# A gated linear recurrence followed by a token and channel mixer: the order of all engines written by a list scheduler inside the kernel

## The chip, the core and the metric

The kernel runs on one core of a Trainium2 chip. Five engines work from queues of their own, each in the order in which the instructions stand in its queue: TensorE (PE) multiplies matrices, VectorE (DVE) and ScalarE (ACT) compute element by element and empty the matmul banks (PSUM), GpSimd (POOL) does slower elementwise work on SBUF and starts the weight transfers, SyncE (SP) starts the other transfers. The metric is the device time of one execution, in microseconds (us). The kernel before takes 209.94 us, the median of 3 runs (209.85 to 210.44).

## The reference

Two stages. First, for each of 4 batches and 8 heads, a recurrence over 768 tokens with a 48 x 48 state; then a mixer over tokens and over the 384 = 8 x 48 channels, with a residual around each half.

```python
for t in range(S):
    state = alpha[:, :, t, :, None] * state + np.einsum('bhd,bhe->bhde', k[:, :, t], v[:, :, t])
    y[:, :, t] = np.einsum('bhd,bhde->bhe', q[:, :, t], state)
...
xt = x.transpose(0, 2, 1)
h = np.maximum(xt @ w_tok1, 0.0) @ w_tok2
u = x + h.transpose(0, 2, 1)
h2 = np.maximum(u @ w_ch1, 0.0) @ w_ch2
return (u + h2).astype(np.float32)
```

The inputs q, k, v and alpha are float32 of 4 x 8 x 768 x 48 each (4.72 MB); the weights are 768 x 256, 256 x 768, 384 x 1536 and 1536 x 384, in float32, turned into bf16 by the transfer.

## The kernel before, in words

The recurrence is computed in chunks of 128 tokens, so that a batch is 6 chunks and the whole is 24 chunks, numbered n. A chunk loads four tiles of 128 x 384 float32 (alpha, k, q, v; `load`, L118 to L127), 196,608 bytes each, in pieces of 48 numbers per token and head, through SP's queue. Its steps are:

- `s_ln` (L129): ACT takes the logarithm of alpha.
- `s_cum` (L134): PE forms the running sums over the chunk with a triangular matrix (one wide matmul L138, four narrow ones L141). ACT forms exp of the sum and of its negative (L144, L146). POOL multiplies k by the latter (L149, tile pkk) and copies v to bf16 (L154, tile vb) and prepares the decay of the chunk for the state (L157, acqm). The product with q (L151, tile pkq) is made by DVE in the first batch and by POOL later.
- `s_tr` (L164): PE transposes pkk and pkq in eight pieces; DVE copies the result to tp in the first batch, ACT later (L171).
- `s_gt` (L174): eight matmuls give each head's 128 x 128 matrix of products; DVE applies the triangular mask (L183, gtm).
- `s_y` (L186): PE updates the state (L193, L196) in the bank pair that L180 uses too, DVE scales it to bf16 (L201), PE forms the output from the masked matrix and from the state of the chunk before (L207, L211), and ACT copies it to x (L215).

When a batch has its six x tiles, its mixer (L222) follows: `tok1` (12 matmuls, L229), `tok2` (12, L238; DVE adds x and gives u, L241), `utp` (18 transposes of u, one group for each block of 128 channels, L247 and L249), `ch1` (72 matmuls, L259, for each of 12 blocks of hidden channels the two halves of the tokens one after the other; ACT empties the first half and DVE the second, L262 and L264) and `ch2` (72 matmuls, L269, then the addition of u on DVE, L272, and the store on SP, L273). All the mixer's matmul groups rotate through three banks; the transposes of u use the bank of the chunk transposes.

The order is written by a loop over the chunks (L309 to L333). It emits the sums of chunk n+1 before the transposes of chunk n, and between the steps of a chunk it takes pieces of the mixer of an earlier batch from a queue, by a count of units. Three `ch2` groups of each batch are held back and put between the steps of the next mixer. The tile framework then orders the instructions further by its own priorities, and inserts the waits.

The transfers have an order of their own. Eight tiles of each input may be in SBUF (NIN = 8). The first chunk of the second batch has its alpha load wait for the copy vb of chunk 5 (L125 and L126). The two token weights are started by POOL after the vb of chunk 4, the two channel weights after that of chunk 5 (L313 to L318); POOL's queue is all that holds them.

## Time and profile before

| what | before |
|---|---|
| median of 3 runs | 209.94 us |
| the profiled execution's own time | 210.22 us |
| its span, first to last instruction | 208.4 us |
| PE busy, share of the span | 174.2 us, 84% |
| DVE busy | 105.0 us, 50% |
| ACT busy | 85.8 us, 41% |
| POOL busy | 62.9 us, 30% |
| HBM read and written | 25.17 MB and 4.72 MB |
| packets under 512 bytes | 100,288 of 106,322 |

The profile shows one execution. Its time is measured from outside, and is 1.8 us longer than the span from the first to the last instruction. The page cuts the span into 40 slices and gives the busy share of each engine in tenths; other views give groups of like instructions with their busy time and their waits, the waits of one engine, the instructions in order of time, and the chain of work that ended last. A line number names the line of the kernel that issued the instruction. Busy times of matmuls overlap, so the time from one start to the next says more of their cost than their own length.

### The profile page before, as it was taken

What the parts mean: (1) busy time and instruction counts of PE and PEld (TensorE: products, weight loads), DVE (VectorE), ACT (ScalarE), POOL (GpSimd) and SP (SyncE); (2) the same over time, 40 slices, a digit from 0 to 9 for tenths busy, and PEclk for the clock granted to TensorE, in tenths of its full rate; (3) what the DMA queues carried; (4) which work ended last, traced back from release to release, by engine and by line L of the source; (5) the groups of instructions that cost most, each with busy time, mean ns of one, the idle gap of its engine ahead of it and who ended that gap; (6) DMA issues with size and microseconds to landing.
All of it is one profiled execution on the core that took longest, in us unless ns stands there. A gap on an engine that the chain in (4) does not pass through costs nothing.

```text
span 208.4 us, 4139 instructions
## 1 busy us (share of the span) xinstructions
PE 174.2 (84%) x1616; PEld 111.5 (53%) x1616; DVE 105.0 (50%) x179; ACT 85.8 (41%) x171; POOL 62.9 (30%) x104
## 2 busy tenths in 40 slices
PE   1276669232799999989999999999999999999993
PEld 0154445111475566646666666667656665656661
DVE  1277554103357455438765664378656446555321
ACT  3442221040526773685167744642667310054000
POOL 2543166004450441583245234551444000000000
PEclk9999999958559999999999999999999999999999
DMA  7999939999999998999989802111100021110132
GB/s 142 220 220 212 182 40 175 208 182 198 191 222 218 188 223 167 226 237 212 235 198 220 165 1 78 39 38 42 38 5 0 35 82 38 40 39 0 38 113 75
DMA packets 106322, 26.99 MB, mean 129 GB/s; under 512 B 100288, under 2 KB 105920, under 8 KB 106304
## 3 DMA queue, kind: packets, MB, share of 16 engines
q1 hardware_dynamic: 103296, 23.60, 53.7%
q0 software_dynamic: 3008, 3.15, 9.2%
q8 instruction: 12, 0.20, 0.4%
q14 instruction: 6, 0.05, 0.1%
HBM read 25.17 MB, written 4.72 MB: 143 GB/s over the span
## 4 chain that ended last, share of the span: by engine, by line
PE 59%; issue 12%; DMA 10%; ACT 8%; POOL 6%; SPq 2%; DVE 1%; POOLq 0%; ACTq 0%
PE ps_mm L269 20%; PE ps_mm L259 19%; DMA at<-in_alpha_dram 10%; ACT tp L171 4%; PE ps_tp L169 4%; PE ps_mm L238 4%; PE gt_ps L180 3%; PE ps_tp L247 2%; PE ps_mm L229 2%; SPq L124 2%; PE ps_y L207 1%; ACT a_sb L144 1%; PE ps_cum L138 1%; PE gt_ps L196 1%; POOL vb L154 1%
## 5 line engine op out<-in xcount | busy, mean ns | idle before, releaser
L259 PE MATMUL ps_mm<-ut,wc_152 128*128 128x384 bf16 x288 | 53.4, 330 | 1.2 <-DVE rt L264 0.5
L269 PE MATMUL ps_mm<-wc_153,rt 128*128 128x384 bf16 x288 | 50.9, 326 | 0.0
L264 DVE TENSOR_SCALAR rt<-ps_mm 128x384 bf16<-128x384 f32 x48 | 26.5, 555 | 22.9 <-PE ps_mm L259 22.6
L183 DVE TENSOR_TENSOR gtm<-gt_ps,u_107 128x1024 bf16<-128x1024 f32 x24 | 29.3, 1220 | 15.7 <-PE gt_ps L180 15.7
L269 PEld LDWEIGHTS <-rt 128*128 128x128 bf16 x288 | 27.1, 98 | 16.9
L259 PEld LDWEIGHTS <-wc_152 128*128 128x128 bf16 x288 | 26.8, 99 | 17.4 <-issue 1.5
L262 ACT ACTIVATE rt<-ps_mm 128x384 bf16<-128x384 f32 x48 | 23.1, 497 | 23.8 <-PE ps_mm L259 23.8
L215 ACT ACTIVATE x_sb<-ps_y 128x384 bf16<-128x384 f32 x24 | 11.8, 492 | 39.3 <-PE ps_y L211 35.2
L272 DVE TENSOR_TENSOR o_sb<-ps_mm,u_sb 128x384 f32<-128x384 f32 x24 | 13.3, 556 | 28.7 <-PE ps_mm L269 28.7
L154 POOL CAST vb<-vt 128x384 bf16<-128x384 f32 x24 | 12.8, 532 | 35.4 <-issue 23.6
L171 ACT COPY tp<-ps_tp 128x1024 bf16<-128x1024 bf16 x18 | 18.3, 1017 | 7.0 <-PE ps_tp L169 6.7
L144 ACT ACTIVATE a_sb<-ps_cum 128x388 f32<-128x388 f32 x24 | 11.9, 495 | 18.6 <-PE ps_cum L141 13.0
L241 DVE TENSOR_TENSOR u_sb<-ps_mm,x_sb 128x384 bf16<-128x384 f32 x24 | 12.0, 550 | 14.2 <-PE ps_mm L238 14.0
L180 PE MATMUL gt_ps<-tp 48*128 48x128 bf16 x192 | 11.9, 241 | 4.6 <-DVE tp L171 2.4
L180 PEld LDWEIGHTS <-tp 48*128 48x128 bf16 x192 | 6.4, 102 | 13.6 <-ACT tp L171 5.9
L146 ACT ACTIVATE ia_sb<-ps_cum 128x384 f32<-128x384 f32 x24 | 11.7, 487 | 0.0
L149 POOL TENSOR_TENSOR pkk_128<-kt,ia_sb 128x384 bf16<-128x384 f32 x8 | 7.9, 993 | 11.7 <-ACT ia_sb L146 11.7
L238 PE MATMUL ps_mm<-ht,wt_151 128*128 128x384 bf16 x48 | 11.4, 374 | 0.0
L229 PE MATMUL ps_mm<-x_sb,wt_150 128*128 128x384 bf16 x48 | 10.1, 342 | 0.6 <-ACT x_sb L215 0.6
L207 PE MATMUL ps_y<-vb,gtm 128*128 128x48 bf16 x192 | 9.6, 192 | 0.9 <-DVE gtm L183 0.9
L151 POOL TENSOR_TENSOR pkq_125<-qt,a_sb 128x384 bf16<-128x384 f32 x6 | 6.0, 996 | 14.3 <-ACT a_sb L144 14.3
L157 POOL TENSOR_TENSOR acqm<-a_sb,bm 128x8 f32<-128x8 f32 x24 | 5.5, 230 | 14.9 <-ACT a_sb L144 13.8
(91 smaller groups left out, 204.3 us busy)
## 6 DMA issues: line engine op xcount, KB each, us to landing
at<-in_alpha_dram SPq DMA_DIRECT2D x24, 192.0 KB, 3.7
kt<-in_k_dram SPq DMA_DIRECT2D x24, 192.0 KB, 3.8
qt<-in_q_dram SPq DMA_DIRECT2D x24, 192.0 KB, 3.8
vt<-in_v_dram SPq DMA_DIRECT2D x24, 192.0 KB, 3.8
out_dram<-o_sb SPq DMA_DIRECT2D x24, 192.0 KB, 1.9
wc_152<-in_moe_w_ch_dram POOLq DMA_DIRECT2D x1, 1152.0 KB, 10.1
wc_153<-in_moe_w_ch_dram POOLq DMA_DIRECT2D x1, 1152.0 KB, 17.2
wt_150<-in_moe_w_tok_dram POOLq DMA_DIRECT2D x1, 384.0 KB, 5.3
```

The source lines that it names most:

```text
L144: act.activation(a_sb, ps_cum[:, 0 : HD + 4], AF.Exp)
L154: gates[n] = gps.tensor_copy(vb, c["vt"])
L171: (act.copy if n >= NCH else dve.tensor_copy)(tp, ps_tp)
L180: pe.matmul(gt_ps[:, 4 * (h % 2) + j, :], lhsT=tp[base : base + D, 4 + j, :], rhs=tp[base : base + D, j, :], start=True, stop=True)
L183: dve.tensor_tensor(gtm, gt_ps, mask_b, ALU.mult)
L229: pe.matmul(ps, lhsT=wt1[:, kc, m * 128 : (m + 1) * 128], rhs=x[kc], start=(kc == 0), stop=(kc == NS - 1))
L238: pe.matmul(ps, lhsT=wt2[:, kc, i * 128 : (i + 1) * 128], rhs=ht[kc], start=(kc == 0), stop=(kc == NDT - 1))
L259: pe.matmul(ps, lhsT=wc1[:, kc, mc * 128 : (mc + 1) * 128], rhs=ut[kc][:, cs], start=(kc == 0), stop=(kc == NM - 1))
L262: act.activation(t[:, cs], ps, AF.Relu)
L264: dve.tensor_scalar_max(t[:, cs], ps, 0.0)
L269: pe.matmul(ps, lhsT=rt[mc][:, i * 128 : (i + 1) * 128], rhs=wc2[:, mc, :], start=(mc == 0), stop=(mc == NDC - 1))
L272: dve.tensor_tensor(t, ps, u[i], ALU.add)
```

## The change

The loop over the chunks, the queue of mixer pieces and the framework's own ordering are taken out. In their place a class `Plan` collects every piece of work as an operation with the engines that may do it and an estimated time on each, the operations that it needs, a priority, and the buffers that it takes and frees. `issue` then walks through a model of the engines: of the operations that can start, it takes the engine whose next start is earliest and on it the one with the best priority, and emits it. The emitted order is final on every engine (`tc.manual_schedule()`); the framework still inserts the waits. In its model PE runs at half speed for the first 36 us, work of other engines counts as ready for PE 0.6 us after its end from then on, and transfers share one wire in order of issue.

With it other things change:

- Alpha and k of chunk n+1 are loaded before q and v of chunk n in the first batch. NIN is 6.
- The first token weight is started after acqm of chunk 4; the second token weight and the first channel weight after vb of chunk 5; the second channel weight after vb of chunk 6.
- A one-column copy on POOL (`hold_back`) from the second token weight into the alpha tile of chunk 6 makes that tile's load, and what follows it on SP, wait until that weight has landed.
- State updates take one of the mixer's three banks, not the bank pair of the masked matrices.
- u is transposed for two token blocks at a time into a mixer bank; the u copies go to DVE or ACT as planned, and so do tp, and the emptying of the banks after `tok1` and `ch1`.
- `ch1` runs over all 12 blocks for the first half of the tokens and then for the second; `tok1` is planned matmul by matmul, `ch2` in parts of four.
- `ch2` groups are no longer held back by hand; priorities place them.

Some of the rings of buffers are a little longer or shorter. The computation of each piece is as before.

```diff
+class Plan:
...
+    LAG = {"PE": 220, "ACT": 180, "DVE": 150, "POOL": 110}
+    def __init__(self, rings, cold, window, slack):
+        self.rings = rings
+        self.cold = cold
+        self.window = window
+        self.slack = slack
+        self.ops = []
+        self.taken = {r: [] for r in rings}
+        self.asked = {r: [] for r in rings}
+        self.mixed = ("pmix", "ptp", "pcum")
+    def op(self, engines, emit, deps=(), prio=0, takes=None, frees=(), lands=0.0):
+        o = {"eng": engines, "emit": emit, "deps": [d for d in deps if d is not None],
+             "prio": (prio, len(self.ops)), "takes": [takes] if isinstance(takes, str) else list(takes or ()), "lands": lands, "users": [],
+             "end": None}
+        for t in frees:
+            t, only = t if isinstance(t, tuple) else (t, None)
+            t["users"].append((o, only))
+        for ring in o["takes"]:
+            self.asked[ring].append(o)
+        self.ops.append(o)
+        return o
+    def issue(self):
+        free = {}
+        wire = 0.0
+        todo = list(self.ops)
+        while todo:
+            ready = []
+            for o in todo:
+                if any(d["end"] is None for d in o["deps"]):
+                    continue
+                at = max((d["end"] for d in o["deps"]), default=0.0)
+                if "PE" in o["eng"] and at > self.cold:
+                    at = max(d["end"] + (0.0 if "PE" in d["eng"] else self.slack)
+                             for d in o["deps"])
+                for ring in o["takes"]:
+                    held = self.taken[ring]
+                    if ring not in self.mixed and o is not next(
+                            p for p in self.asked[ring] if p["end"] is None):
+                        at = 1e12
+                    if len(held) >= self.rings[ring]:
+                        at = max([at] + [u["end"] or 1e12 for u, only in
+                                         held[-self.rings[ring]]["users"] if only in (None, ring)])
+                if at >= 1e12:
+                    continue
+                ways = []
+                for e, ns in o["eng"].items():
+                    start = max(at, free.get(e, 0.0))
+                    slow = 2.0 if e == "PE" and start < self.cold else 1.0
+                    ways.append((start + ns * slow, start, e))
+                done, start, eng = min(ways)
+                ready.append((start, o["prio"], eng, done, o))
+            assert ready, "a ring is too small"
+            eng = min(ready, key=lambda r: r[:2])[2]
+            mine = [r for r in ready if r[2] == eng]
+            limit = min(r[0] for r in mine) + self.window.get(eng, 0.0)
+            start, _, _, done, o = min((r for r in mine if r[0] <= limit), key=lambda r: (r[1], r[0]))
+            todo.remove(o)
+            free[eng], o["start"] = done, start
+            if o["lands"]:
+                wire = max(wire, start + 1650.0) + o["lands"]
+                o["end"] = wire + 900.0
+            else:
+                o["end"] = done + self.LAG.get(eng, 0)
+            for ring in o["takes"]:
+                self.taken[ring].append(o)
+            o["emit"](eng)
...
+    plan = Plan({"loads": NT * 4, "at": NIN, "kt": NIN, "qt": NIN, "vt": NIN, "la": NLA, "a": NAUX,
+                 "ia": NAUX, "pkq": NPK, "pkk": NPK, "vb": NAUX, "acqm": NAUX, "tp": NGT,
+                 "gtm": NGT, "ss": NSS, "x": 18, "ht": 4, "u": 12, "ut": 2, "rt": NRT,
+                 "o": 6, "pcum": 1, "ptp": 1, "pgt": 1, "py": 1, "pmix": NMIX}, 36000.0, {"PE": 0.0}, 600.0)
...
-    def after(ins, gate, cls=mybir.DependencyClass.Sync):
-        tc.add_manual_dep(ins.ins, gate.ins.name,
-                          mybir.DependencyInfo(cls, mybir.DependencyReason.DATA),
-                          reason="transfer order")
-        return ins
-
-    def load_weight(dst, src, gate):
-        after(gps.dma_start(dst, src.rearrange("(c p) m -> p c m", p=128)), gate,
-              mybir.DependencyClass.NoSync)
...
+    def weight(name, dst, src, after):
+        def emit(e):
+            gps.dma_start(dst, src.rearrange("(c p) m -> p c m", p=128))
+        wload[name] = plan.op({"POOL": 1000}, emit, [after], prio=-1,
+                              lands=dst.shape[1] * dst.shape[2] * 512 / 350.0)
...
+        loads[n][name] = plan.op({"SP": 550}, emit, [after], takes=[name, "loads"], lands=196608 / RATE)
...
+    def hold_back(landed, issued):
+        def emit(e):
+            c = tiles[NCH]
+            c["at"] = inp.tile([128, H, D], F32, name="at")
+            gps.tensor_copy(c["at"][:, 0, 0:1], wt2[:, 0, 0:1])
+        return plan.op({"POOL": 70}, emit, [landed, issued], -1)
...
+        def e_tp(e):
+            c["tp"] = gtp.tile([128, 8, 128], BF16, name="tp")
+            (dve.tensor_copy if e == "DVE" else act.copy)(c["tp"], c["ptp"])
+        tp = plan.op({"DVE": 600, "ACT": 905}, e_tp, [trk, trq], P, takes="tp", frees=[trk])
...
+            def e_su(e):
+                ps = c["s"] = ps_mix_p.tile([128, HD], F32, name="ps_mm")
+                if ci > 0:
+                    pe.matmul(ps[:, 0:HD], lhsT=idd2, rhs=s_prev, start=True, stop=False,
+                              skip_group_check=True)
+                for j in range(4):
+                    pe.matmul(ps[:, 96 * j : 96 * j + 96],
+                              lhsT=pkk_t[n % NPK][:, 2 * j : 2 * j + 2, :],
+                              rhs=c["vb"][:, 2 * j : 2 * j + 2, :],
+                              start=(ci == 0 and j == 0), stop=(j == 3), skip_group_check=True)
+            su = plan.op({"PE": 330 if ci else 170}, e_su, [pkk, vb, s_dep], P, takes="pmix",
+                         frees=[pkk, vb] + ([s_dep] if ci else []))
...
+            def e_utp(e, g=g, hold=hold):
+                hold["ps"] = ps_mix_p.tile([128, 6, 128], BF16, name="ps_mm")
+                for j in range(NM):
+                    for i in range(2):
+                        pe.transpose(hold["ps"][:, 2 * j + i, :],
+                                     u[2 * g + i][:, j * 128 : (j + 1) * 128], id128)
+            tj = plan.op({"PE": 330}, e_utp, us[2 * g : 2 * g + 2], TOK,
+                         takes="pmix" if g else ["pmix", "ut"])
+
+            def e_ut(e, g=g, hold=hold):
+                if g == 0:
+                    ut_t[0] = utpool.tile([128, NM, S], BF16, name="ut")
+                (dve.tensor_copy if e == "DVE" else act.copy)(
+                    ut_t[0][:, :, g * 256 : g * 256 + 256],
+                    hold["ps"].rearrange("p (j i) t -> p j (i t)", i=2))
+            uts.append(plan.op({"DVE": 470, "ACT": 700}, e_ut, [tj], TOK,
+                               frees=[(tj, "pmix")]))
+            if g == 0:
+                ut_op = tj
...
+        rts, heads = [], []
+        for half in range(2):
+            cs = slice(half * 384, half * 384 + 384)
...
+                c1 = plan.op({"PE": 3 * MM}, e_ch1,
+                             (uts if half else uts[0:2]) + [wload["wc1"]] + heads[-1:],
+                             CH1, takes=["pmix"] if half else ["pmix", "rt"],
+                             frees=[(ut_op, "ut")])
+
+                def e_rt(e, mc=mc, cs=cs, hold=hold):
+                    evac(e, rt[mc][:, cs], hold["ps"])
+                rts.append(plan.op(EV, e_rt, [c1], CH1, frees=[(c1, "pmix")]))
+                heads.append(c1)
...
+            first = prev = None
+            for part in range(3):
+                prev = plan.op({"PE": 4 * MM}, lambda e, part=part, f=e_ch2: f(e, part),
+                               rts + [wload["wc2"], prev], CH2 - (0.05 if part else 0),
+                               takes=None if part else "pmix",
+                               frees=[(h, "rt") for h in heads[:NDC]])
+                first = first or prev
...
-        for n in range(NT):
-            b, ci = divmod(n, NCH)
-            if n + 1 < NT:
-                s_cum(n + 1)
-            if n + 1 == NCH - 2:
-                load_weight(wt1, moe_w_tok1, gates[n + 1])
-                load_weight(wt2, moe_w_tok2, gates[n + 1])
-            if n + 1 == NCH - 1:
-                load_weight(wc1, moe_w_ch1, gates[n + 1])
-                load_weight(wc2, moe_w_ch2, gates[n + 1])
-            while n + 1 >= NCH - 1 and loaded < min(NT, n + 1 + AHEAD):
-                load(loaded)
-                loaded += 1
-            if n + 2 < NT:
-                s_ln(n + 2)
-            s_tr(n)
-            over = fill(10 + over)
-            s_gt(n)
-            over = fill(10 + over)
-            s_y(n)
-            over = fill(9 + over)
-            if ci == NCH - 1:
-                fill(1000)
-                add_mixer(b)
-                over = 0
...
+    load_ak(0)
+    for n in range(NT):
+        if n + 1 < NCH:
+            load_ak(n + 1)
+        if n < NCH:
+            load_qv(n)
+        pkk, vb, acqm = chunk(n)
+        if n == NCH - 2:
+            weight("wt1", wt1, moe_w_tok1, acqm)
+        if n == NCH - 1:
+            weight("wt2", wt2, moe_w_tok2, vb)
+            weight("wc1", wc1, moe_w_ch1, vb)
+        if n == NCH:
+            weight("wc2", wc2, moe_w_ch2, vb)
+        if NCH - 1 <= n < NT - 1:
+            load_ak(n + 1, hold_back(wload["wt2"], wload["wc1"]) if n == NCH - 1 else None)
+            load_qv(n + 1)
+        if n % NCH == NCH - 1 and n >= NCH:
+            mixer(n // NCH - 1)
+    mixer(B - 1)
+    with tc.manual_schedule():
+        plan.issue()
```

375 lines of the change are left out of this document (195 added, 180 removed).

## The prediction

> **What bounds the kernel now.** I read the page's slices first, then the same span cut into stretches where the picture changes, then the waits of POOL, SP and TensorE inside the bad stretch, and last the chain of waits.
>
> ```profile
> span 208.4 us, 4139 instructions
> PE   1276669232799999989999999999999999999993
> PEclk9999999958559999999999999999999999999999
> DMA  7999939999999998999989802111100021110132
> GB/s 142 220 220 212 182 40 175 208 182 198 191 222 218 188 223 167 226 237 212 235 198 220 165 1 78 39 38 42 38 5 0 35 82 38 40 39 0 38 113 75
> ```
>
> Each digit is 5.21 us. To slice 7 TensorE (PE) is part idle, slices 7 and 8 show 2 and 3, and slices 8 and 10 to 11 have a lowered clock. DMA is at 9 nearly everywhere to slice 22 and then falls away. So the early part waits for data, the later part for PE. The stretches (columns: busy us of PE, PE weight loads, DVE, ACT, POOL, then granted clock, DMA share, GB/s) say it in numbers:
>
> ```profile
> 0.00:35.00 35.00, 19.46 (x203) 14.36 (x204) 17.44 (x37) 11.59 (x24) 16.03 (x32) 1.00 0.94 171
> 35.00:41.80 6.80, 2.60 (x29) 1.26 (x28) 1.82 (x2) 0.49 (x1) 0.05 (x1) 1.00 1.09 193
> 41.80:65.00 23.20, 14.17 (x104) 8.87 (x104) 7.80 (x14) 8.49 (x17) 8.27 (x13) 0.63 1.13 201
> 65.00:205.00 140.00, 137.96 (x1284) 87.03 (x1281) 77.36 (x127) 65.22 (x129) 38.59 (x59) 1.00 0.46 106
> ```
>
> From 65 to 205 us PE is busy for 137.96 of 140 us: it shortens only by denser PE work, or by work done before it begins. Before 65 us it is busy for 36 of 65, much of it at half speed. What is left of its work at 65, and what was done by then (the groups of PE, first after 65 and then before 65):
>
> ```profile
> L269 PE MATMUL ps_mm<-wc_153,rt 128*128 128x384 bf16 x288 | 50.9, 326 | 0.0
> L259 PE MATMUL ps_mm<-ut,wc_152 128*128 128x384 bf16 x275 | 49.6, 326 | 0.7 <-ACT rt L262 0.3
> L238 PE MATMUL ps_mm<-ht,wt_151 128*128 128x384 bf16 x36 | 7.2, 325 | 0.0
> L229 PE MATMUL ps_mm<-x_sb,wt_150 128*128 128x384 bf16 x36 | 6.8, 326 | 0.1
> ...
> L180 PE MATMUL gt_ps<-tp 48*128 48x128 bf16 x64 | 4.4, 283 | 3.9 <-DVE tp L171 2.4 <-ACT tp L171 1.1 <-DVE ss_131 L201 0.4
> L259 PE MATMUL ps_mm<-ut,wc_152 128*128 128x384 bf16 x15 | 4.3, 405 | 0.5 <-DVE rt L264 0.5
> L207 PE MATMUL ps_y<-vb,gtm 128*128 128x48 bf16 x56 | 3.5, 213 | 0.9 <-DVE gtm L183 0.9
> ```
>
> Seven of 24 recurrence chunks had their output (L207 has eight per chunk), eight their L180; of batch 0's mixer, the two token stages and 15 of its 72 first channel matmuls were done. The end, and the cost of one dense matmul, from the chain:
>
> ```profile
> 193.35 11.71 PE ps_mm L269 x72
> 205.09 0.56 DVE o_sb L272
> ```
>
> 72 matmuls in 11.71 us are 0.163 us each. After PE's end near 205.1 come 3.3 us of last addition, store and shutdown. The 635 large matmuls left at 65 us take 635 x 0.163 = 103.3 us; the other 36.8 us of the 140.1 are some 16.5 chunks and 54 u transposes. These are nine times the six transposes that the trace gives 0.44 us, so 4.0 us:
>
> ```profile
> 140.92 0.44 PE ps_tp L247 x6
> ```
>
> That leaves (36.8 - 4.0) / 16.5 = 2.0 us per chunk, small stalls included.
>
> Why the first 65 us are thin shows on POOL, on SP's queue and on PE:
>
> ```profile
> 15.48 0.84 POOL L154 CAST vb<-vt 128x384 bf16<-128x384 f32 x1
> 27.73 1.00 POOL L112 DMA_DIRECT2D wt_150<-in_moe_w_tok_dram  x1
> 32.76 0.50 POOL L154 CAST vb<-vt 128x384 bf16<-128x384 f32 x1
> 33.20 0.80 POOL L112 DMA_DIRECT2D wc_152<-in_moe_w_ch_dram  x1
> 34.00 1.05 POOL L112 DMA_DIRECT2D wc_153<-in_moe_w_ch_dram  x1
> ```
>
> ```profile
> 34.39 6.29 SPq L124 DMA_DIRECT2D at<-in_alpha_dram  x1
> 40.73 5.00 SPq L124 DMA_DIRECT2D kt<-in_k_dram  x1
> 45.78 4.33 SPq L124 DMA_DIRECT2D qt<-in_q_dram  x1
> 50.15 1.57 SPq L124 DMA_DIRECT2D vt<-in_v_dram  x1
> 51.82 0.63 SPq L124 DMA_DIRECT2D at<-in_alpha_dram  x1
> ```
>
> ```profile
> 37.46 0.37 PE L207 MATMUL ps_y<-vb,gtm 128*128 128x48 bf16 x8 [0.89 <-DVE gtm L183]
> 45.00 0.48 PE L138 MATMUL ps_cum<-la_123,u_107 128*128 128x384 bf16 x1 [5.93 <-ACT la_123 L132]
> 52.53 0.48 PE L138 MATMUL ps_cum<-la_124,u_107 128*128 128x384 bf16 x1 [4.07 <-ACT la_124 L132]
> 59.23 1.17 PE L259 MATMUL ps_mm<-ut,wc_152 128*128 128x384 bf16 x3
> ```
>
> The value copy vb of chunk 2 runs at 15.5, that of chunk 5 at 32.8: 5.8 us per chunk, while batch 0's inputs could be there much sooner (24 tiles of 196,608 bytes at the slices' 212 to 220 GB/s are 0.91 us each, 22 us in all, from about 2 us). Both channel weights go out behind that last vb. Then the input queue crawls: four input issues take 6.29 + 5.00 + 4.33 + 1.57 = 17.2 us where one takes 0.63 later. PE puts out chunk 5's output at 37.46, 4.7 us after its vb, and its cumulative sums then stand 5.9 us for chunk 6's alpha and 4.1 us for chunk 7's; the first channel matmuls come at 59.23.
>
> ```profile
> at<-in_alpha_dram SPq DMA_DIRECT2D x24, 192.0 KB, 3.7
> wc_152<-in_moe_w_ch_dram POOLq DMA_DIRECT2D x1, 1152.0 KB, 10.1
> wt_150<-in_moe_w_tok_dram POOLq DMA_DIRECT2D x1, 384.0 KB, 5.3
> 34.39 17.55 DMA at<-in_alpha_dram
> ```
>
> An alpha tile lands after 3.7 us in the median, but 17.55 us when the weights fly. Between 35.0 and 41.8 us nearly all traffic is weights, at 193 GB/s, so a channel weight (1.18 MB as landed) takes 6.1 us alone and a token weight 2.0.
>
> **The change, part by part.**
>
> (1) First batch. Alpha and k come a chunk ahead, ACT and POOL are ordered by readiness, and POOL no longer meets chunk 5's vb behind late sums. Chunks can then follow their inputs at 4 x 0.91 = 3.6 us. PE is at half speed there: eight gt matmuls take 0.61 us early, against 0.33 to their successor late. (The clock row reads full there; I go by the durations.)
>
> ```profile
> 14.77 0.61 PE L180 MATMUL gt_ps<-tp 48*128 48x128 bf16 x8 [0.40 <-DVE ss_131 L201]
> 132.99 0.33 PE gt_ps L180 x8
> ```
>
> Twice the 2.0 us that a chunk costs late is 4.0 us, and the stalls in it need not double: it fits, just about, with PE next in line. The first token weight now goes out behind chunk 4's acqm, near 19 us, into the input stream; I charge 3 us for it (2.0 of transfer, and a slower mixture). The last v of batch 0 lands near 2 + 22 + 3 = 27 us, vb near 27.5, instead of 32.8 to 33.3. Bounds: no gain (vb at 33), or 24 us if the weight costs nothing.
>
> (2) Weights and hold. The second token weight and the first channel weight go out near 28 and 29. By wt_150's 5.3 us to landing, the former lands at 32 to 33 and the latter near 38. The 70 ns POOL copy makes chunk 6's alpha wait for the former; what stands behind it on POOL is chunk 6's own work, which needs that alpha. On SP it holds all later loads, but the channel weight fills the wire meanwhile. PE has token work to about 38 and then starts the first channel stage, which in the trace starts at 59.23. So no wait for alpha 6 of 5.9 us. Chunk 6's four tiles land at about 39 to 42.
>
> (3) The second channel weight goes out behind chunk 6's vb, about 42.5, moving from about 44.5. Here I see the price. The SP rows show that weights in flight leave inputs about 4 tiles in 17 us; for one weight that is about 8 us and 1 to 2 tiles. So chunk 7's q or v, and all of chunk 8, come only after 52. The planner counts otherwise: its single wire serves transfers in order of issue, 914 ns a load, and with 550 ns an issue it has some 20 loads issued before that weight. In its reckoning chunk 8's alpha lands near 45 and the weight near 62. It therefore writes chunk 8's sum into PE's order near 47, with about half of the first channel stage (36 matmuls, 5.9 us) still behind it, and the second channel stage after chunk 10. PE takes its queue in order, so it stands from about 47 until alpha 8 lands near 53: 7 us. Behind it stand those 36 matmuls, then the evacuations on ACT and DVE, and POOL's pkk. The clock will fall, as it did in the stretch 41.8 to 65 (0.63). Bounds of this wait: 0, if the order gives PE enough to do, and 12, twice the 5.9 us seen.
>
> The Trainium skill (DMA: Bandwidth & Descriptors, section Queues, rings and completion order) says that each DMA engine takes turns between its queues by packet, not by issue order. The crawling SP rows agree with that, and it speaks against this part of the change; by the planner's own first-come wire the sum would be rival one's.
>
> (4) After 53, inputs come at 0.91 us a tile: chunk 10 complete at 53 + 12 x 0.91 = 64, its chain of sums, transposes and mask 5 us more, as from chunk 5's vb to its output. So PE becomes full at about 69 us, with 11 chunks and all 72 first channel matmuls done. Against the old state at 65 that is 57 x 0.163 = 9.3 us and 3.4 chunks x 2.0 = 6.8 us of PE work, 16.1 in all.
>
> (5) From there on, tp and rt may go to DVE or ACT, whichever the planner finds free, and state updates leave the gt banks. The idle time in 65 to 205 is 2.0 us; I take all of it as gained. Bounds: 4 gained, twice that, as stalls too short to show as idle may lie in the 2.0 us per chunk, or 3 lost, 0.16 us, one matmul, at each of the 20 state updates (they now take one of the three mixer banks for an estimated 0.3 us of PE (a wide matmul of 0.163 and four narrow ones) and a DVE pass the size of the last addition's 0.56, 17 us of bank time in all, hidden while two others serve PE). The u transposes stay 72, the u copies 12 of equal size, and the larger memset count lies before the first alpha: nothing, hidden under the same work.
>
> **Sum.** PE full from 69, remaining 140.1 - 16.1 - 2.0 = 122.0, end 191.0, plus 3.3: a span of 194.3. The profiled execution took 210.2 against its span of 208.4, 1.8 more, so 196.1; the median of the runs is 0.3 under that execution: 195.8, said as 196.
>
> **Rivals.**
>
> *One, no stand at chunk 8.* PE is full from 38.5 on. By then it has 6 chunks and the token stages, against the old state 1.6 chunks (3.2 us) and 15 matmuls (2.4) less: 38.5 + 140.1 + 5.6 - 2.0 + 3.3 = 185.5, and 187 as a median. For it: 72 channel matmuls (11.7 us) are a large cover. Against it: the crawling queue. 22%.
>
> *Two, the first batch keeps its 5.8 us per chunk,* since half-speed PE just fits and the order is fixed. Everything from the weights on comes 5.5 us later: 201.5. For it: the 0.61 us gt rows; against: the waits on POOL are for late sums, not for PE's speed. 18%.
>
> *Three, slower.* Output stores share SP's queue with the loads, and in the written order a store stands until its sum is ready; loads behind it wait. Batch 2's and batch 3's inputs would each come late by the stretch that one second channel stage takes, 11.7 us, or more. If PE then stood 8 us or more at each of the two, 196 + 16 = 212. It decides from 14 us of such waits. For it: fixed orders on SP and PE. Against it: loads are planned many microseconds ahead of stores. 6%.
>
> *Four, no effect.* The hold only moves the wait, and early gains come back as late stalls: 210. 4%.
>
> **How the numbers follow.** My forecast, 196, has 50%. 185 to 204 holds the forecast with its bounds, most of rival one and nearly all of rival two; below it lies a denser late stretch, above it rivals three and four and a longer stand: some 20%. A difference under 0.3% can't be told from none. Faster: 50 + 22 + 18 = 90%; within 0.3% nearly all of rival four's 4%; slower 6%.
>
> **What will show it.** Step 1: chunk 5's vb at 27 to 28 us. Step 2: channel matmuls from about 38 and no PE wait for chunk 6 over 2 us. Step 3: a PE wait of about 7 us near 47 to 54 with a lowered clock, and SP issues of several us while the second channel weight flies. Step 4: PE full from about 69. Step 5: PE busy above 98.5% from there. It is wrong if PE waits repeatedly for inputs after 75 us, or if chunk 5 ends after 34.

## The result, and the profile after

The changed kernel takes 200.84 us in the median (197.92 to 202.14); the kernel before, run beside it, takes 210.19 (209.85 to 210.56). The ratio is 0.948, with a 95% interval of 0.936 to 0.960. The ratio is that of the two faster runs of the changed kernel, 197.92 and 200.74 us, since the other two lie over 1.5% above the fastest; by the medians it is 0.956. The forecast was 196 with a range of 185 to 204: the direction and the range hold, the point is 4.8 us too low. The profiled execution took 200.74 us for a span of 198.6.

First the slices of the changed kernel, each of 4.97 us, as they stand on its page:

```profile
span 198.6 us, 4154 instructions
PE   1487686789629999999999897999999999999993
PEclk9999859969985999999999999999999999999999
GB/s 130 212 196 198 170 128 125 210 191 200 184 183 201 216 202 202 202 176 222 253 188 181 211 175 152 5 2 83 131 28 0 3 0 0 79 83 79 32 127 79
```

The hole of before (2 and 3 in slices 7 and 8, at 36 to 47 us) has gone. A smaller one has come in slices 10 and 11 (6 and 2, at 50 to 60 us), and the clock row shows 8 and 5 just behind it. From 65 us on PE is at 9 nearly everywhere, as before. The same stretches as those of the prediction, with one more for the late part (busy us of PE, PE weight loads, DVE, ACT, POOL, then clock, DMA share, GB/s), of the changed kernel and then of the kernel before:

```profile
0.00:35.00 35.00, 21.93 (x233) 15.04 (x234) 18.47 (x40) 13.38 (x27) 14.19 (x32) 0.90 0.91 166
35.00:41.80 6.80, 4.68 (x34) 2.54 (x32) 3.99 (x8) 0.92 (x2) 0.00 (x0) 0.93 1.05 205
41.80:65.00 23.20, 17.42 (x156) 10.77 (x155) 6.92 (x11) 13.71 (x30) 10.33 (x16) 0.80 1.10 192
65.00:190.00 125.00, 122.42 (x1168) 79.07 (x1167) 58.94 (x92) 65.98 (x140) 37.21 (x58) 1.00 0.52 116
```

```profile
65.00:190.00 125.00, 122.96 (x1193) 78.18 (x1191) 72.30 (x118) 63.28 (x126) 38.59 (x59) 1.00 0.50 111
```

Up to 65 us PE is busy for 21.93 + 4.68 + 17.42 = 44.0 us, against 36.2 before. Behind 65 us its share has not risen: 97.9% against 98.4%. What was left of its work at 65 us says the same in matmuls (groups of PE in the changed kernel, after 65 us, and the one group of the first channel stage before 65 us):

```profile
L471 PE MATMUL ps_mm<-wc_157,rt 128*128 128x384 bf16 x288 | 48.9, 326 | 0.0
L453 PE MATMUL ps_mm<-ut,wc_156 128*128 128x384 bf16 x233 | 43.7, 326 | 1.1 <-DVE ss_133 L330 0.7 <-ACT rt L363 0.3
L405 PE MATMUL ps_mm<-ht,wt_155 128*128 128x384 bf16 x36 | 7.8, 326 | 0.4 <-DVE ss_133 L330 0.4
L381 PE MATMUL ps_mm<-x_sb,wt_154 128*128 128x384 bf16 x36 | 7.6, 326 | 0.0
L303 PE MATMUL gt_ps<-tp 48*128 48x128 bf16 x120 | 6.0, 218 | 0.1
L341 PE MATMUL ps_y<-vb,gtm 128*128 128x48 bf16 x128 | 5.8, 183 | 0.0
...
L453 PE MATMUL ps_mm<-ut,wc_156 128*128 128x384 bf16 x57 | 13.2, 384 | 2.1 <-DMA wc_156<-in_moe_w_ch_dram 1.9 <-ACT rt L363 0.2
```

593 large matmuls are left (288 + 233 + 36 + 36), where before there were 635: 42 x 0.163 = 6.8 us. Chunks left are 15.5 (120 and 128 by eight, the mean), where there were 16.5: another 2.0 us. So 8.8 us of work have moved ahead of 65 us. The two spans differ by 208.4 - 198.6 = 9.8 us, which leaves 1.0 us to everything behind 65 us.

Next POOL and SP of the changed kernel, the rows that the steps of the prediction named (start, length, engine, line, operation, the idle time before it and what ended that):

```profile
28.68 0.50 POOL L270 CAST vb<-vt 128x384 bf16<-128x384 f32 x1 [1.99 <-DMA vt<-in_v_dram]
...
29.29 0.76 POOL L190 DMA_DIRECT2D wt_155<-in_moe_w_tok_dram  x1
...
34.53 0.18 POOL L216 CAST at<-wt_155 128x1 f32<-128x1 bf16 x1 [3.73 <-DMA wt_155<-in_moe_w_tok_dram]
44.64 0.51 POOL L270 CAST vb<-vt 128x384 bf16<-128x384 f32 x1 [9.92 <-DMA vt<-in_v_dram]
...
46.37 1.07 POOL L190 DMA_DIRECT2D wc_157<-in_moe_w_ch_dram  x1
...
53.62 0.99 POOL L258 TENSOR_TENSOR pkk_129<-kt,ia_sb 128x384 bf16<-128x384 f32 x1 [2.48 <-DMA kt<-in_k_dram]
58.61 0.99 POOL L262 TENSOR_TENSOR pkq_125<-qt,a_sb 128x384 bf16<-128x384 f32 x1 [4.00 <-DMA qt<-in_q_dram]
```

```profile
49.88 4.29 SPq L209 DMA_DIRECT2D at<-in_alpha_dram  x1
54.22 4.12 SPq L209 DMA_DIRECT2D kt<-in_k_dram  x1
```

The copy vb of chunk 5 runs at 28.68, not at 32.76. The second channel weight wc_157 is issued at 46.37 and lands 12.5 us later (the page's list of issues), at 58.9. While it flies, SP's input issues take 4.29 and 4.12 us where 0.63 us stands in the quieter row of before, POOL gets chunk 8's k only at 53.6 and its q at 58.6, and the chain of waits shows the alpha tile of chunk 9 under way for 10.48 us:

```profile
49.88 10.48 DMA at<-in_alpha_dram
```

PE in that stretch, rows of its timeline:

```profile
40.62 3.80 PE L453 MATMUL ps_mm<-ut,wc_156 128*128 128x384 bf16 x12 [1.91 <-DMA wc_156<-in_moe_w_ch_dram]
...
54.66 0.40 PE L286 MATMUL ps_tp<-id_112,pkk_129 128*128 128x128 bf16 x4 [1.91 <-POOL pkk_129 L258]
...
59.66 0.61 PE L291 MATMUL ps_tp<-id_112,pkq_125 128*128 128x128 bf16 x4 [3.58 <-POOL pkq_125 L262]
...
61.44 2.08 PE L453 MATMUL ps_mm<-ut,wc_156 128*128 128x384 bf16 x6
...
66.33 0.36 PE L341 MATMUL ps_y<-vb,gtm 128*128 128x48 bf16 x8
...
68.39 0.81 PE L471 MATMUL ps_mm<-wc_157,rt 128*128 128x384 bf16 x4
```

The first channel matmuls start at 40.62, where they started at 59.23 before. The first twelve take 3.64 us to their successor, 0.30 us each, since the clock is at half there (0.50 from 41 to 44 us). Then PE stands twice for chunk 8, 1.91 and 3.58 us, and behind that works at half speed: six channel matmuls take 2.08 us at 61.44, which is some 0.33 us each against the usual 0.163.

### The profile page after: what moved, and what is told of

The parts are those of the page before. It is cut to its first block, busy times and chain, and to the rows that moved or that the text cites. A ratio compares the mean times of both kernels' runs of the same rounds, so it can differ in the third digit from the quotient of the medians.

```text
span 198.6 us, 4154 instructions
## 1 busy us (share of the span) xinstructions
PE 171.7 (86%) x1616; PEld 110.4 (56%) x1616; DVE 90.6 (46%) x154; ACT 94.0 (47%) x198; POOL 61.7 (31%) x105
## 4 chain that ended last, share of the span: by engine, by line
PE 56%; DMA 24%; SPq 10%; ACT 5%; issue 2%; DVE 1%; POOL 0%; ACTq 0%; POOLq 0%; DVEq 0%
PE ps_mm L471 24%; PE ps_mm L453 20%; DMA at<-in_alpha_dram 16%; SPq L209 10%; DMA wc_156<-in_moe_w_ch_dram 5%; DMA vt<-in_v_dram 3%; PE ps_mm L381 2%; PE ps_mm L405 2%; PE gt_ps L303 2%; ACT tp L296 1%; PE ps_y L341 1%; PE ps_tp L286 1%; PE ps_cum L240 1%; PE ps_y L346 1%; ACT ia_sb L249 1%
## 5 line engine op out<-in xcount | busy, mean ns | idle before, releaser
L453 PE MATMUL ps_mm<-ut,wc_156 128*128 128x384 bf16 x288 | 56.4, 337 | 3.2 <-DMA wc_156<-in_moe_w_ch_dram 1.9
L363 ACT ACTIVATE rt<-ps_mm 128x384 bf16<-128x384 f32 x84 | 40.3, 493 | 22.1 <-PE ps_mm L453 21.4
L471 PE MATMUL ps_mm<-wc_157,rt 128*128 128x384 bf16 x288 | 48.9, 326 | 0.0
L270 POOL CAST vb<-vt 128x384 bf16<-128x384 f32 x24 | 12.1, 504 | 28.2 <-DMA vt<-in_v_dram 22.0
L296 DVE COPY tp<-ps_tp 128x1024 bf16<-128x1024 bf16 x16 | 10.9, 684 | 5.6 <-PE ps_tp L291 5.6
L405 PE MATMUL ps_mm<-ht,wt_155 128*128 128x384 bf16 x48 | 10.3, 326 | 1.6 <-DMA wt_155<-in_moe_w_tok_dram 1.2
L365 DVE TENSOR_SCALAR rt<-ps_mm 128x384 bf16<-128x384 f32 x12 | 6.6, 554 | 10.7 <-PE ps_mm L453 10.5
L303 PE MATMUL gt_ps<-tp 48*128 48x128 bf16 x192 | 10.8, 240 | 0.1
L258 POOL TENSOR_TENSOR pkk_129<-kt,ia_sb 128x384 bf16<-128x384 f32 x6 | 6.0, 997 | 13.6 <-ACT ia_sb L249 11.1
L341 PEld LDWEIGHTS <-gtm 128*128 128x128 bf16 x192 | 8.2, 101 | 3.4 <-DVE gtm L309 1.5
L296 ACT COPY tp<-ps_tp 128x1024 bf16<-128x1024 bf16 x8 | 8.1, 1018 | 2.5 <-PE ps_tp L291 2.5
## 6 DMA issues: line engine op xcount, KB each, us to landing
wc_156<-in_moe_w_ch_dram POOLq DMA_DIRECT2D x1, 1152.0 KB, 10.5
wc_157<-in_moe_w_ch_dram POOLq DMA_DIRECT2D x1, 1152.0 KB, 12.5
```

The source lines that it names most:

```text
L296: (dve.tensor_copy if e == "DVE" else act.copy)(c["tp"], c["ptp"])
L303: pe.matmul(gt[:, 4 * (h % 2) + j, :], lhsT=c["tp"][base : base + D, 4 + j, :], rhs=c["tp"][base : base + D, j, :], start=True, stop=True)
L341: pe.matmul(ps[:, h, :], lhsT=c["gtm"][:, 4 * (h % 2) + h // 2, :], rhs=c["vb"][:, h, :], start=(h == 0), stop=(ci == 0 and h == H - 1), s ...
L363: act.activation(dst, ps, AF.Relu)
L405: pe.matmul(hold["ps"], lhsT=wt2[:, kc, i * 128 : (i + 1) * 128], rhs=ht[kc], start=(kc == 0), stop=(kc == NDT - 1))
L453: pe.matmul(hold["ps"], lhsT=wc1[:, kc, mc * 128 : (mc + 1) * 128], rhs=ut_t[0][:, kc, cs], start=(kc == 0), stop=(kc == NM - 1))
```

## The experiments

Each compares with the kernel before, run beside it (209.5 to 209.6 us in the median in all of them). Each expectation was written ahead of its run, and says itself what its theories A, B and C stand for; the letters do not mean the same in all of them.

### The changed kernel again, and three ways round the collision

The control is the changed kernel as it is.

> The changed kernel once more, beside the three that follow on the same chip. Both theories: about 200.8 us, since its four runs lay between 197.9 and 202.1, and PE waits of 5 to 6 us for chunk 8's inputs between 52 and 60 us.

It took 198.29 us (196.94 to 199.11), ratio 0.945 (0.940 to 0.950). This is 2.5 us under the median above; the ratios, 0.945 and 0.948, agree. PE stands for chunk 8 once here:

```profile
59.16 0.37 PE L321 MATMUL ps_mm<-vb,pkk 128*128 128x96 bf16 x4 [4.11 <-POOL vb L270]
```

The control is the figure to which the others compare.

The first edit loads one twelfth of the second channel weight and multiplies with that block in every place. All orders stay.

```diff
-            gps.dma_start(dst, src.rearrange("(c p) m -> p c m", p=128))
+            w = src.rearrange("(c p) m -> p c m", p=128)
+            if name == "wc2":
+                gps.dma_start(dst[:, 0:1, :], w[:, 0:1, :])
+            else:
+                gps.dma_start(dst, w)
...
-   pe.matmul(hold["ps"], lhsT=rt[mc][:, i * 128 : (i + 1) * 128], rhs=wc2[:, mc, :],
+   pe.matmul(hold["ps"], lhsT=rt[mc][:, i * 128 : (i + 1) * 128], rhs=wc2[:, 0, :],
```

> Left out: 11 of the 12 blocks of the second channel weight are not loaded, and every matmul of the second channel stage multiplies with the first block. The order of all engines is unchanged. Theory A, the transfer of that weight starves chunk 8's inputs and PE stands in its fixed order behind them: the PE waits of 1.9 and 3.6 us near 53 to 60 go, the clock stays full there, and of the 8.5 us of PE time lost between 50 and 65 us some 7 come back: about 193 us. Theory B, the stand comes from the fixed order alone, whatever the wire carries: waits of 4 us or more stay, about 200 us. Theory C, the wire is what bounds to 125 us, and the time comes back later as waits for batches 2 and 3: the early waits go, but the time stays above 197.

It took 191.89 us (189.62 to 192.84), ratio 0.908 (0.902 to 0.915): 6.4 us under the control, and the two intervals are far apart. The stretch 50 to 65 us in the control, and then in this kernel:

```profile
50.00:65.00 15.00, 10.47 (x117) 6.75 (x116) 5.94 (x8) 7.85 (x16) 6.05 (x10) 0.89 1.12 192
```

```profile
50.00:65.00 15.00, 14.09 (x163) 9.15 (x161) 8.40 (x11) 10.90 (x24) 6.78 (x12) 1.00 1.04 206
```

PE is busy for 14.09 instead of 10.47 us, at the full clock instead of 0.89, and issues 163 matmul records instead of 117. Every engine's order is that of the control, so the transfer of that weight costs 6.4 us here, close to what theory A said (193 us). The edit takes the bytes away and not only their place, so it does not say what moving them is worth. It is no version to use, since that weight is needed.

The next two move the collision instead. In one the planner lets a load start only when the load four before it has landed:

```diff
+    flying = [None] * 4
...
-        loads[n][name] = plan.op({"SP": 550}, emit, [after], takes=[name, "loads"], lands=196608 / RATE)
+        loads[n][name] = plan.op({"SP": 550}, emit, [after, flying[-4]], takes=[name, "loads"], lands=196608 / RATE)
+        flying.append(loads[n][name])
```

> In the planner's model an input load starts only when the load four before it has landed, which is how the SP queue behaves in the trace; so the planner sees the second channel weight land some 13 us earlier and the loads of chunks 8 to 11 behind it. The transfers themselves are issued in the same order. Theory A: PE's order now has first and second channel matmuls where the inputs are late, the waits between 50 and 60 us shrink to 2 us or less in sum, and the time falls by 4 to 7 us, to about 195. Theory B: the order is no better for a better model of the wire, no change. Theory C: 198 to 200, with new waits later.

In the other the second channel weight goes out right behind the first one, and all loads of the second batch stand behind both in the plan:

```diff
-        if n == NCH:
             weight("wc2", wc2, moe_w_ch2, vb)
-            load_ak(n + 1, hold_back(wload["wt2"], wload["wc1"]) if n == NCH - 1 else None)
+            load_ak(n + 1, hold_back(wload["wt2"], wload["wc2"]) if n == NCH - 1 else None)
```

> The second channel weight is started right behind the first, after chunk 5's vb, and before any load of the second batch. Theory A: the weight flies from about 38 to 45 us, while PE has the first channel stage as cover (11.7 us from about 40.6), and the inputs of chunks 6 to 11 follow without a break; PE is nearly full from 41 us, and the time falls by 5 to 8 us, to about 194. Theory B: no change. Theory C: 198 to 200, because chunk 11 still comes as late as before.

They took 198.44 us (197.77 to 202.55), ratio 0.945 (0.940 to 0.950), and 197.47 us (196.44 to 198.22), ratio 0.941 (0.937 to 0.946). Neither can be told from the control, and the 195 and 194 us of theory A did not come. PE in two stretches, 41.8 to 65 us and 75 to 115 us, in the control, then with four loads in flight, then with wc2 first:

```profile
41.80:65.00 23.20, 18.48 (x169) 11.35 (x167) 7.99 (x11) 13.88 (x30) 11.47 (x17) 0.84 1.10 195
...
75.00:115.00 40.00, 38.95 (x486) 26.57 (x485) 29.45 (x46) 24.75 (x54) 23.95 (x39) 1.00 1.00 209
```

```profile
41.80:65.00 23.20, 20.76 (x218) 13.30 (x218) 9.12 (x13) 16.82 (x38) 11.81 (x18) 1.00 1.14 200
...
75.00:115.00 40.00, 35.39 (x427) 23.06 (x426) 25.29 (x39) 25.90 (x57) 23.24 (x36) 1.00 1.01 203
```

```profile
41.80:65.00 23.20, 21.36 (x197) 13.01 (x196) 9.55 (x14) 15.86 (x35) 9.78 (x15) 0.95 1.07 196
...
75.00:115.00 40.00, 36.66 (x465) 24.64 (x462) 26.63 (x40) 26.85 (x60) 24.15 (x37) 1.00 1.01 212
```

In the first stretch PE is busy for 2.3 and 2.9 us more than in the control, at a higher clock; in the second for 3.6 and 2.3 us less. What was won early was given back later. Data, stores included, move at 203 to 212 GB/s in all three, about as fast as in the control. The reading is that PE, having caught up with them, waits in an order that was written for faster ones: the planner takes 196,608 bytes as 914 ns, which is 215 GB/s, while in the kernel with wc2 first the alpha tiles of chunks 12 to 23 are used 4.25 us apart, which is 185 GB/s of input.

### The planner's wire

That reading has a test: the kernel with wc2 first, and the planner told 195 GB/s for the loads from the second batch on.

```diff
-        loads[n][name] = plan.op({"SP": 550}, emit, [after], takes=[name, "loads"], lands=196608 / RATE)
+        loads[n][name] = plan.op({"SP": 550}, emit, [after], takes=[name, "loads"],
+                                 lands=196608 / (RATE if n < NCH else 195.0))
```

> As the run with the second channel weight first, and the planner is told 195 instead of 215 GB/s for the loads of batches 2 to 4, so that it writes each chunk's steps later into PE's order. In that earlier run chunk 12 to 23's alpha came 4.25 us apart, against 3.96 in the planner's reckoning, and PE lost 4 us more than the changed kernel between 80 and 105 us. Theory C, the planner's wire is too fast: this loss goes, 192 to 195 us. Theory C wrong, PE's later losses have another cause: no change from 197.5.

It took 194.89 us (194.63 to 195.54), ratio 0.931 (0.927 to 0.934). This is 2.6 us under the kernel that differs from it in that number alone, with intervals that do not touch, and the best of all complete kernels: it beats both the kernel before and the changed one. PE in the stretch 50 to 65 us, and 75 to 115 us:

```profile
50.00:65.00 15.00, 12.93 (x153) 8.31 (x154) 8.02 (x12) 8.28 (x19) 9.54 (x15) 1.00 1.03 203
...
75.00:115.00 40.00, 37.70 (x475) 25.53 (x473) 28.18 (x43) 26.52 (x58) 23.51 (x38) 1.00 1.01 212
```

It keeps most of the early gain (12.93 against the control's 10.47) and gives back 1.25 us later (37.70 against 38.95), where with the fast wire it was 2.3. Between the two kernels the transfers and their gates are the same; the order of the work differs, that of the stores among SP's loads and the choice between DVE and ACT included. So the result fits the reading, but only one rate was tried, and that a new order moves the time by itself is not ruled out.

A last step from there starts the three weights behind pkk of chunk 5 and not behind its vb, since data hardly move from 28 to 31 us:

```diff
-            weight("wt2", wt2, moe_w_tok2, vb)
-            weight("wc1", wc1, moe_w_ch1, vb)
-            weight("wc2", wc2, moe_w_ch2, vb)
+            weight("wt2", wt2, moe_w_tok2, pkk)
+            weight("wc1", wc1, moe_w_ch1, pkk)
+            weight("wc2", wc2, moe_w_ch2, pkk)
```

> As the run with the slower wire, and the second token weight and both channel weights are started behind chunk 5's pkk instead of its vb, some 2 to 3 us sooner, to fill the gap of 2 to 3 us in which no transfer runs near 28 to 31 us. Theory: the wire is what bounds until 40 us, so 1.5 to 2.5 us shorter, 192.5 to 193.5. Rival, the weights starve the last v of batch 0, whose chunk then ends later, and PE starts the channel stage no sooner: 195 or more.

It took 195.59 us (193.44 to 197.03), ratio 0.930 (0.923 to 0.937): nothing gained over the kernel without it, where 1.5 to 2.5 us were expected. The edit also did less than it says. POOL issues the second token weight here at 28.95, and without the edit at 29.56:

```profile
28.95 0.76 POOL L190 DMA_DIRECT2D wt<-in_moe_w_tok_dram  x1
```

```profile
29.56 0.76 POOL L190 DMA_DIRECT2D wt<-in_moe_w_tok_dram  x1
```

The gap of the wire stays (0 GB/s from 28 to 30 us), so what it is worth stays open.

### The parts of the change, one at a time

The hold without the weight: the one-column copy reads vb of chunk 5 and not the second token weight.

```diff
-            gps.tensor_copy(c["at"][:, 0, 0:1], wt2[:, 0, 0:1])
+            gps.tensor_copy(c["at"][:, 0, 0:1], tiles[NCH - 1]["vb"][:, 0, 0:1])
...
-            load_ak(n + 1, hold_back(wload["wt2"], wload["wc1"]) if n == NCH - 1 else None)
+            load_ak(n + 1, hold_back(vb, wload["wc1"]) if n == NCH - 1 else None)
```

> The hold on the second batch's loads is undone: the one-column copy into chunk 6's alpha tile reads chunk 5's vb, as the wait before the change did, and no longer the second token weight. The order on all engines is that of the changed kernel, and only the moment differs at which SP may go on, near 30 us and not near 34.7. Theory A, two queues share the wire by packets: chunk 6's alpha now moves beside both weights, the second token weight lands up to 1 us later, chunk 6's inputs at about the same time as they did, and the time stays within 1 us of the changed kernel's. Rival, the hold is worth its name: weights land 3 us later or more, PE's waits for them grow, 2 to 4 us slower.

It took 198.36 us (197.40 to 199.36), ratio 0.947 (0.942 to 0.951). All engines keep the control's order. The copy now runs at 28.98 instead of 34.53, and the time is that of the control: holding the second batch's loads behind the weight itself is worth nothing that can be measured here.

The state updates back in the bank pair of the masked matrices:

```diff
-                ps = c["s"] = ps_mix_p.tile([128, HD], F32, name="ps_mm")
+                ps = c["s"] = ps_gt_p.tile([128, 1024], F32, name="gt_ps")
...
-            su = plan.op({"PE": 330 if ci else 170}, e_su, [pkk, vb, s_dep], P, takes="pmix",
+            su = plan.op({"PE": 330 if ci else 170}, e_su, [pkk, vb, s_dep], P, takes="pgt",
```

> The state updates go back to the bank pair of the masked matrices; the planner orders everything anew with that. My prediction put this part at zero: within 1 us of the changed kernel. Rival: the shared pair makes each chunk's products wait for the scaling of the state before them, some 0.2 us for each of 20 chunks, 2 to 4 us slower.

It took 198.78 us (197.99 to 199.03), ratio 0.948 (0.945 to 0.952), 0.5 us from the control and inside its interval: no effect shown.

The transposes of u by blocks of channels, in the bank of the chunk transposes, as the kernel before has them:

```diff
-        for g in range(NS // 2):
+        for j in range(NM):
...
-                hold["ps"] = ps_mix_p.tile([128, 6, 128], BF16, name="ps_mm")
+                hold["ps"] = ps_tp_p.tile([128, 8, 128], BF16, name="ps_tp")
...
-                             (uts if half else uts[0:2]) + [wload["wc1"]] + heads[-1:],
+                             uts + [wload["wc1"]] + heads[-1:],
```

> One part undone: u is transposed by channel blocks as before, into the bank of the chunk transposes, so that the first channel stage waits for all three u copies and not for two of three; the planner orders everything anew. My prediction put this part at zero: within 1 us of the changed kernel (198.3 on the chip of the first four runs). Rival: the transposes of u and of the chunks now wait for each other in the one bank, 0.5 us or more for each of 12 groups, 4 us slower or more.

It took 203.46 us (202.38 to 205.76), ratio 0.975 (0.967 to 0.982), some 5 us more than the control. In the order that the planner writes for it, the state updates of chunks 18 and 19 stand ahead of the outputs of chunks 16 and 17, which read the same two slots. Those two chunks are computed from later states, with the same count of instructions, so this too is no version to use. PE's longest wait while the second channel weight flies, for an alpha tile, is 6.27 us in one piece, where the control's is 4.11:

```profile
59.37 0.48 PE L240 MATMUL ps_cum<-la,u 128*128 128x384 bf16 x1 [6.27 <-ACT la L234]
```

So the pairs of token blocks may be worth up to 5 us, but this does not show it: the edit rewrote the whole order, and 2.2 us of the difference stand in that one wait.

### Order against transfers

The change's transfers in the kernel before, with its own loop and the framework's ordering: alpha and k ahead, the weights' new places, and the hold.

```diff
-    def load(n):
+    def load(n, part=AK + QV):
...
-                after(d, gates[NCH - 1])
+                gps.tensor_copy(t[:, 0, 0:1], wt2[:, 0, 0:1])
...
-                load_weight(wt1, moe_w_tok1, gates[n + 1])
-                load_weight(wt2, moe_w_tok2, gates[n + 1])
+                load_weight(wt1, moe_w_tok1, acq_gate[n + 1])
...
```

> The kernel before, with the change's transfers alone: alpha and k a chunk ahead in the first batch, the first token weight behind acqm of chunk 4, the second token weight and the first channel weight behind vb of chunk 5, the second channel weight behind vb of chunk 6, and chunk 6's alpha held until the second token weight has landed. The loop, its queue of mixer pieces and the framework's ordering stay. Theory A, the transfers alone bring what the change brings to 65 us: 201 to 204 us. Rival, POOL and PE stand in the old order (chunk 5's vb at 32.8 behind late sums), and the new transfers cannot start sooner: 208 us or more.

It took 211.39 us (210.46 to 212.01), ratio 1.008 (1.004 to 1.011): the transfers alone make it a little slower. Its PE still meets the sums of chunks 6 and 7 first and the channel matmuls after them:

```profile
51.55 0.48 PE L142 MATMUL ps_cum<-la,u 128*128 128x384 bf16 x1 [3.65 <-ACT la L136]
54.85 0.48 PE L142 MATMUL ps_cum<-la,u 128*128 128x384 bf16 x1 [2.74 <-ACT la L136]
...
60.55 1.17 PE L263 MATMUL ps_mm<-ut,wc 128*128 128x384 bf16 x3
```

The other way round, the change with the framework free to reorder what the planner wrote:

```diff
-    with tc.manual_schedule():
-        plan.issue()
+    plan.issue()
```

> The planner's order is only the order in which the pieces are handed over; the framework's own ordering is on again and may move instructions. Theory A, the gain to 65 us comes from the order of loads, weights and POOL and ACT work, and what is handed over is mostly kept: 198 to 203 us. Rival, the final order is what the gain rests on: 205 us or more.

It took 208.62 us (207.09 to 211.51), ratio 0.995 (0.992 to 0.999): nearly all of the gain is gone. Its POOL shows why (the first, third and last of its four weight issues; then one of SP's):

```profile
1.62 1.01 POOL L190 DMA_DIRECT2D wt<-in_moe_w_tok_dram  x1
...
14.07 0.80 POOL L190 DMA_DIRECT2D wc<-in_moe_w_ch_dram  x1
19.82 1.08 POOL L190 DMA_DIRECT2D wc<-in_moe_w_ch_dram  x1
```

```profile
18.14 6.44 SPq L209 DMA_DIRECT2D vt<-in_v_dram  x1
```

The framework moves the weights ahead on POOL, and the first batch's inputs starve. The kernel with that undone alone, each weight tied in order (no wait) behind the POOL operation that the plan puts ahead of it:

```diff
-    def weight(name, dst, src, after):
+    def weight(name, dst, src, after, gate):
...
+            g = tiles[gate[0]][gate[1]]
+            tc.add_manual_dep(d.ins, g.ins.name,
+                              mybir.DependencyInfo(mybir.DependencyClass.NoSync, mybir.DependencyReason.DATA),
+                              reason="transfer order")
...
-    with tc.manual_schedule():
-        plan.issue()
+    plan.issue()
```

> The framework's ordering on again, as in the run that took 208.6 us, but each weight's start is pinned behind the POOL instruction that it follows in the changed kernel. In that earlier run the weights were moved up to 1.6, 12.2, 14.1 and 19.8 us and starved the first batch's inputs. Theory A, that was all that the framework's ordering cost: 198 to 201 us. Rival, the final order on PE and the others is what the gain rests on: 205 us or more.

It took 199.92 us (199.56 to 201.80), ratio 0.956 (0.950 to 0.962). Two rows of it, chunk 5's vb (two copies in one piece) and the start of the channel matmuls:

```profile
31.83 0.95 POOL L274 CAST vb<-vt 128x384 bf16<-128x384 f32 x2
```

```profile
50.74 2.95 PE L457 MATMUL ps_mm<-ut,wc 128*128 128x384 bf16 x9
```

The first batch here keeps about the pace of the kernel before (vb at 31.83 instead of 28.68), yet the time is within 1.6 us of the control, and the intervals of the two ratios just touch (0.950). What this kernel does otherwise than the one that has the transfers alone shows in what PE does while the weights fly: its channel matmuls start at 50.74, and not at 60.55, with nearly the same starts of the weights (that kernel issues its first channel weight at 35.06, this one at 33.49). So the transfers without the rest are worth nothing, and the rest with the weights ahead of the inputs 0.5%; together, even in the framework's ordering, they bring 4.4%. Two things were not tried: the planner's order with the transfers of before, and the other parts of the change (pairs of u blocks, the choice between DVE and ACT) apart from the order, so that it is the order of the mixer's work on PE is argued from the rows and not shown. The fixed order of the engines beyond that, and with it the faster first batch, are worth some 1.6 us by the medians and 2.3 by the ratios (0.0108 of 209.6).

## Why the prediction was right, and where it was off

**Step 1, the first batch: right.** vb of chunk 5 was put at 27.5 and ran at 28.68 (32.76 before), inside the bounds and near the value taken. The reading of half speed was rough: 0.61 us is the length of eight products and 0.33 us a time to the successor; as lengths they are 0.61 and 0.40 (at 26.84 and 21.59 us in the changed kernel). What the step is worth is smaller than it suggests: rival two gave 201.5 us if the first batch kept its pace, and the kernel with pinned weights, which about keeps it, takes 199.92 against the control's 198.29.

**Step 2, weights and hold: the waits right, the landings late.** No PE wait for chunk 6 shows; the waits there are 1.91 us for the first channel weight and, by the list of waits, 1.2 us for the second token weight. But the latter landed at 34.5 (32 to 33 was said), the former at 40.6 (38), and chunk 6's v at 44.6 (39 to 42). The second token weight was issued at 29.29 and not near 28; from its issue to the hold's copy it took 5.2 us, as counted (5.3). The channel weight was issued at 30.04 and took 10.5 us, where some 9 were counted. Near the issues, from 28 to 30 us, the wire is empty, as the rows of 2 us below show: 2 GB/s. The hold was credited with letting the weights through; held behind vb alone the time is the same.

**Step 3, the stand: right in kind and size, a little off in place.** 7 us were forecast; taking the transfer away gains 6.4. It was to be PE's sum waiting for chunk 8's alpha from 47 to 54. In the trace that alpha is there in time, since the second channel weight was issued at 46.37 and not at 42.5, and PE waits for chunk 8's k and q instead, in the transposes, from about 53 to 60: 1.91 + 3.58 = 5.5 us, with the half clock behind it. That the two sums agree so well is in part luck, since the victim, the moment and the number of waits differ. Rival one, no stand, fell: its price of 9 us for the stand is the right order, and the kernel with a twelfth of the weight, at 191.9, is the nearest to it, 5 us over its 187. The Trainium skill (DMA: Bandwidth & Descriptors, section Queues, rings and completion order) has the DMA engines take turns between queues by packet, and the SP rows of 4.29 and 4.12 us agree with it again.

**Step 4, the state when PE is full: this is the step that failed.** At 69 us it was to have 11 chunks and all 72 first channel matmuls, 16.1 us of work more than before at 65, so 12.1 us net of the 4 us later. (Eleven chunks less 7.5 are 3.5 and not 3.4, which would make it 0.2 more.) By the trace all 72 are done by 68.39, where the second stage begins, but at 66.33 only the ninth chunk's output is formed. At 65 us 8.8 us of work are ahead. The difference of 3.3 us is the term that was mis-sized. Its cause, by the rows, is in steps 2 and 3: the second channel weight has landed at 58.9 and not at 52.5, and chunk 8's last inputs come some 6 us later than the 53 from which step 4 counts. The half clock under the first twelve channel matmuls, 3.64 - 12 x 0.163 = 1.7 us, was in no term either; how the 3.3 us divide was not measured.

**Step 5, the late stretch: not as put.** All of the 2.0 us of idle time were taken as gained. None of it was: from 65 to 190 us PE is idle for 125.00 - 122.42 = 2.6 us, and its share is 97.9% and not over 98.5%. The 1.0 us left over for this stretch has another source, which no row names; it lies within what the estimate of 2.0 us a chunk leaves open. The bound on the mixer banks that the state updates now take shows, once: a channel matmul waits 0.70 us for the scaling of a state,

```profile
122.87 0.65 PE L453 MATMUL ps_mm<-ut,wc_156 128*128 128x384 bf16 x3 [0.70 <-DVE ss_133 L330]
```

and with 0.4 us for a token matmul this is all of that kind in the groups above. The kernel with the updates back in their old banks takes as long, so nothing that can be measured is won or lost by that part.

**The sum.** 210.2 - 196.1 = 14.1 us were forecast on the profiled executions, 210.22 - 200.74 = 9.5 us came: 3.3 of the difference is step 4, 1.0 step 5, and 0.3 the time outside the span, 2.1 us where 1.8 was taken. Rivals three and four fell: no PE wait behind 75 us is for an input held up by a store, and the gain is real. What the prediction saw only as one mistake of the planner, the first-come wire against one weight, seems to be a larger one: the inputs come more slowly than the 215 GB/s it counts with, and with 195 GB/s the kernel was 2.6 us faster once the weight was out of the way. It was not among the rivals. What is left open is what the order is worth without the new transfers, what the pairs of u transposes are worth, and what the empty wire at 28 to 30 us costs.

## What to carry to other kernels

A written order and the transfers that it assumes belong together: here the new transfers without the order gave nothing, and the planned pieces in the framework's ordering, with the weights moved ahead of the inputs, gave 0.5% of the 5%. When an order is computed from a model of the transfers, compare the model's landings with those of the trace and put the measured rate in early; here an order written for data that come too early gave back late what it had won early. A large transfer in a second queue took the wire from a stream of small ones here, so look in the stream for its victim, some tiles behind the last one already issued.

## What the runs showed of the hardware that was not expected

The clock fell without a long stand. In the changed kernel PE's longest idle time between 20 and 26 us is 1.08 us, and the clock is at half from 24 to 30 us, for two of those stretches with PE busy throughout (stretches of 2 us, columns as above):

```profile
22.00:24.00 2.00, 0.72 (x10) 0.45 (x10) 0.62 (x2) 1.72 (x4) 0.96 (x2) 0.93 0.92 163
24.00:26.00 2.00, 1.14 (x9) 0.76 (x10) 1.82 (x3) 0.00 (x0) 0.76 (x2) 0.50 1.32 218
26.00:28.00 2.00, 2.00 (x31) 1.66 (x29) 2.00 (x3) 0.49 (x1) 0.69 (x1) 0.50 1.20 193
28.00:30.00 2.00, 2.00 (x26) 1.41 (x24) 1.31 (x2) 0.27 (x1) 1.32 (x3) 0.50 0.01 2
```

Before 20 us the clock row reads full, but the products are as slow as at half: eight take 0.61 us at 18.23, 0.40 at 21.59 and 0.61 again at 26.84. So the clock was full between 20 and 24 us only, and in the 2 us before the fall PE is busy for 0.72 us, in pieces. The Trainium skill (TensorE: Matmul & The Clock Gate, section What's actually happening) puts the fall after an idle window of some 3.4 us. Here no single idle time was a third of that, so a thin stretch was enough. The fall in the stand from 56 to 60 us differs from it too: the granted clock reads 0.85 from 57.5 to 58.0 us and 0.50 from there on, less than 2 us into the 3.58 us, and in the 3.5 us up to 58.0 PE was busy for 1.41 us.

Whether the order makes the time less steady is not shown. The four runs of the changed kernel lie between 197.92 and 202.14 us, but those of its control between 196.94 and 199.11, and nine runs of the kernel before on one chip between 208.86 and 210.69. The profile of the changed kernel and that of the control, with the same order on every engine, differ in how long PE waits for chunk 8: 1.91 and 3.58 us in the one, 4.11 us in the other.
